# Which queue issues the last three stores of a kernel

## The chip, the cores and the metric

The kernel runs on one core of one Trainium2 chip. Five engines work side by side on it: TensorE (PE in the profile, with its weight loads as PEld), VectorE (DVE), ScalarE (ACT), GpSimd (POOL) and SyncE (SP). Transfers between the chip's memory (HBM) and the core's working memory (SBUF) are DMAs: an engine issues one from its own stream of instructions, and the packets are then moved by 16 DMA engines. In this kernel SP issues nearly all of them (queue q1 in the profile) and ACT a few (q10).

The metric is the device time of one execution in microseconds (us). A profiled execution also has a span, from its first instruction to its last, which is a little shorter than its time.

## The reference

From x of 2048 rows and 640 columns, in bf16, the result is the sum of x and two branches that share one layer norm:

```python
xn = _layernorm(x)
return x + _A_ref(xn, A_wqkv, A_wo) + _B_ref(xn, B_w_gate, B_w_up, B_w_down)

# A: 32 heads of 20, each row sees itself and the 255 rows before it
qkv = (x @ wqkv).reshape(B, S, 3, H, Dh)
scores = einsum("bhqd,bhkd->bhqk", q, k) * (Dh ** -0.5)   # masked to the window
o = einsum("bhqk,bhkd->bhqd", softmax(scores), v)
A = o.reshape(B, S, D) @ wo

# B: 1536 hidden columns
h = sigmoid(xn @ w_gate) * (xn @ w_up)
B = h @ w_down
```

## The kernel before

The 2048 rows are worked in four chunks of 512, and a chunk in four row blocks of 128. For each chunk the kernel normalises and transposes the rows, projects q, k and v, forms the scores and their exponentials in steps, multiplies them with v, and computes the gated branch into tiles `h`. The order of all instructions is written out by hand (`tc.manual_schedule()`): the main loop (lines 757 to 778) interleaves the score steps with other work that it pulls from a list, so that TensorE always has something to do. The output of the first three chunks is part of that list.

The output of the last chunk stands behind the loop, from line 782 on, and the change lies there. The output of a row block needs, for each cut of its columns, twelve matmuls of `h` with the down weights (`down`, line 470) and five of the attention result with `wo` (`add_wo`, line 477), all summed in one bank of PSUM, the memory that TensorE writes. `add_x` (line 481) is one VectorE instruction that halves the sum and adds x, in place, in the tile that holds x's rows. `store` (line 493) then writes those columns to `out` on a queue that it is given. For the first three row blocks the cuts are two halves of 320 columns, and one store of 160 KB on SP's queue takes both (`outp`). The tile of the last row block is not called `rows` in the profile, but `xn`: it lies in the buffer `xns["last"]`, whose rows ACT loads some 20 us before the end (line 790).

The last row block has three cuts, of 320, 256 and 64 columns (line 800), and each is added and stored by itself as soon as its sum is there: 80 KB, 64 KB and 16 KB. The twelve `down` matmuls of the first two cuts are issued ahead of time (lines 808 and 809), those of the third inside the loop. That loop, lines 812 to 817, names the queue of each store. An engine works through its instructions in order, so a store waits on its engine both for the data and for whatever the engine has ahead of it.

After the stores the program ends (the profile's line 841): SP waits for the outstanding stores one after the other, drains, and the engines meet.

Of the kernel before, what the change touches and what calls it, by code (L numbers as in the profile page):

```python
# [93 lines left out]
def kernel(  # L94
# [11 lines left out]
    nc = tc.nc  # L106
# [368 lines left out]
    def add_wo(c, s, y, cut):  # L475
        for m in range(DC):
            nc.tensor.matmul(y[:, 0:cut[1] - cut[0]], lhsT=oc[c, m][:, s * P:(s + 1) * P],  # L477
                             rhs=wo[:, m, cut[0]:cut[1]], start=False, stop=(m == DC - 1))

    def add_x(y, cut, rows):  # L480
        nc.vector.scalar_tensor_tensor(  # L481
            out=rows[:, cut[0]:cut[1]], in0=y[:, 0:cut[1] - cut[0]], scalar=0.5,
            in1=rows[:, cut[0]:cut[1]], op0=MULT, op1=ADD)
# [7 lines left out]
    def store(c, s, rows, cut=(0, D), queue=nc.sync):  # L491
        sb = c * SBC + s
        queue.dma_start(out=out2[sb * P:(sb + 1) * P, cut[0]:cut[1]], in_=rows[:, cut[0]:cut[1]])

    def outp(c, s, ys, rows):
        for y, cut in zip(ys, HALVES):
            add_wo(c, s, y, cut)
        for y, cut in zip(ys, HALVES):
            add_x(y, cut, rows)
        store(c, s, rows)  # L500
# [251 lines left out]
    cuts = [(ends[n, NG - 2] + 2 + n, f"out{n}") for n in range(NCH - 1)] + [(len(todo), None)]  # L752
# [42 lines left out]
    def add_down(s, cut, home, tag):  # L795
        ys[s, cut] = home.tile([P, CW], FP32, name="y0", tag=tag)
        run(down(c, s, ys[s, cut], cut))

    last = SBC - 1
    cuts = (HALVES[0], (HALF, D - U), (D - U, D))  # L800
# [8 lines left out]
    add_down(last, cuts[1], ps_d, "d")  # L809
    for s in range(1, last):  # L810
        outp(c, s, [ys[s, cut] for cut in HALVES], rows[s])
    for cut, queue in zip(cuts, (nc.scalar, nc.sync, nc.scalar)):
        if cut == cuts[2]:
            add_down(last, cut, ps_y, "y")
        add_wo(c, last, ys[last, cut], cut)
        add_x(ys[last, cut], cut, rows[last])
        store(c, last, rows[last], cut, queue)
# [28 lines left out]
```

## Time and profile before

| | |
|---|---|
| three runs | 308.06, 308.20 and 308.88 us, median 308.2 |
| the profiled execution | 308.24 us |
| its span, first to last instruction | 306.4 us |
| granted TensorE clock over the span | 1.00 |
| PE busy | 302.0 us, 99% of the span |
| ACT busy | 198.5 us, 65% |
| DVE busy | 177.7 us, 58% |
| POOL busy | 177.5 us, 58% |
| stores of the last row block | `out_dram<-xn`, 80 KB on ACT's queue, 64 KB on SP's, 16 KB on ACT's |

In the profile a line such as `303.07 0.35 ACTq L493 DMA_DIRECT2D out_dram<-xn x1` is a DMA that ACT issued from line 493: it started at 303.07 us from the span's start, and the issue (not the transfer) occupied ACT's stream for 0.35 us. `SPq` is the same for SP. `out_dram<-xn` says that `out` is written from the tile `xn`. An `EVENT_SEMAPHORE` is an instruction that waits for, or sets, a counter through which engines and DMAs tell each other that something is done; its time is shown once the wait is over. A line of the waits, `SPq L841 <- DMA out_dram<-xn: 0.4, 2, 0.2`, says that SP's stream waited at line 841 for DMAs of that kind, 0.4 us in all, twice, 0.2 us at the longest. In the DMA view a line such as `q10 hardware_dynamic: 8, 0.00, 12.5%` gives a queue's packets in a window, their megabytes, and the share of 16 engines' time that they took; `q8` and `q14` (kind `instruction`) are fetches of the program itself.

### The profile page before, as it was taken

What the parts mean: (1) busy time and instruction counts of PE and PEld (TensorE: products, weight loads), DVE (VectorE), ACT (ScalarE), POOL (GpSimd) and SP (SyncE); (2) the same over time, 40 slices, a digit from 0 to 9 for tenths busy, and PEclk for the clock granted to TensorE, in tenths of its full rate; (3) what the DMA queues carried; (4) which work ended last, traced back from release to release, by engine and by line L of the source; (5) the groups of instructions that cost most, each with busy time, mean ns of one, the idle gap of its engine ahead of it and who ended that gap; (6) DMA issues with size and microseconds to landing.
All of it is one profiled execution on the core that took longest, in us unless ns stands there. A gap on an engine that the chain in (4) does not pass through costs nothing.

```text
span 306.4 us, 10028 instructions
## 1 busy us (share of the span) xinstructions
PE 302.0 (99%) x4314; PEld 164.8 (54%) x4314; DVE 177.7 (58%) x355; ACT 198.5 (65%) x197; POOL 177.5 (58%) x317
## 2 busy tenths in 40 slices
PE   7999999999999999999999999999999999999996
PEld 3654444445657644554457654554546664444774
DVE  5735539879675564497946464483733526372534
ACT  6933877698854649888674647878585547778000
POOL 3174686787982828576682728557382847557000
PEclk9999999999999999999999999999999999999999
DMA  7998987986537062810036212740000210000202
GB/s 206 361 325 266 303 199 213 318 229 192 175 97 166 21 180 70 273 40 2 2 132 131 66 58 87 231 144 0 2 2 2 71 40 25 2 2 2 88 21 68
DMA packets 40174, 36.87 MB, mean 120 GB/s; under 512 B 8864, under 2 KB 39840, under 8 KB 40096
## 3 DMA queue, kind: packets, MB, share of 16 engines
q1 hardware_dynamic: 39264, 35.46, 38.2%
q10 hardware_dynamic: 864, 0.75, 0.8%
q8 instruction: 34, 0.56, 0.8%
q14 instruction: 12, 0.10, 0.1%
HBM read 25.59 MB, written 11.44 MB: 121 GB/s over the span
## 4 chain that ended last, share of the span: by engine, by line
PE 97%; DMA 1%; ACT 1%; DVE 0%; SPq 0%; issue 0%
PE y L470 18%; PE pu L456 18%; PE pg L449 17%; PE pqk L324 15%; PE ps L526 9%; PE pv L353 7%; PE y L477 7%; PE acc L559 6%; DMA xc<-in_A_x_dram 1%; PE pt L277 0%; ACT xn L656 0%; ACT xn L661 0%; DVE xn L667 0%; SPq L156 0%; ACT rstd L662 0%
## 5 line engine op out<-in xcount | busy, mean ns | idle before, releaser
L543 POOL TENSOR_SCALAR_AFFINE_SELECT pT<-pT 64x512 bf16<-64x512 bf16 (+1 forms) x256 | 157.4, 615 | 83.0 <-ACT pT L532 70.5
L532 ACT ACTIVATE pT<-ps 128x2048 bf16<-128x2048 f32 (+1 forms) x76 | 141.0, 1855 | 59.4 <-PE ps L526 56.0
L460 DVE SCALAR_TENSOR_TENSOR h<-th,pu 128x512 bf16<-128x512 f32 x48 | 32.6, 680 | 49.7 <-PE pu L456 44.2
L456 PE MATMUL pu<-xnT,wu 128*128 128x512 bf16 x240 | 59.8, 380 | 0.0
L449 PE MATMUL pg<-xnT,wg 128*128 128x512 bf16 x240 | 59.8, 380 | 0.0
L470 PE MATMUL y<-wd,h 128*128 128x320 bf16 (+2 forms) x396 | 56.6, 295 | 0.0
L470 PEld LDWEIGHTS <-h 128*128 128x128 bf16 x396 | 36.7, 98 | 15.8 <-issue 1.8
L452 ACT ACTIVATE th<-pg 128x512 f32<-128x512 f32 x48 | 28.6, 595 | 15.5 <-PE pg L449 15.4
L449 PEld LDWEIGHTS <-wg 128*128 128x128 bf16 x240 | 22.2, 98 | 25.8 <-issue 1.8
L456 PEld LDWEIGHTS <-wu 128*128 128x128 bf16 x240 | 22.0, 98 | 25.5 <-issue 2.0
L526 PE MATMUL ps<-qT,kT 20*64 20x320 bf16 (+4 forms) x1440 | 32.1, 260 | 0.0
L571 DVE STREAM_TRANSPOSE t<-acc 128x512 f32<-128x512 f32 x32 | 21.1, 696 | 17.3 <-PE acc L559 17.3
L526 PEld LDWEIGHTS <-kT 20*64 20x64 bf16 x1440 | 15.4, 103 | 25.0 <-issue 22.4
L481 DVE SCALAR_TENSOR_TENSOR rows<-y,rows 128x320 bf16<-128x320 f32 x30 | 14.5, 488 | 22.8 <-PE y L477 22.7
L583 DVE TENSOR_TENSOR on<-t,rec 128x320 bf16<-128x320 f32 (+4 forms) x48 | 26.1, 543 | 1.1
L353 PE MATMUL pv<-wv,xnT 128*128 128x320 bf16 x160 | 25.7, 300 | 0.0
L477 PE MATMUL y<-wo,oc 128*128 128x320 bf16 (+2 forms) x165 | 24.2, 295 | 0.0
L324 PE MATMUL pqk<-xnT,wq 128*128 128x512 bf16 x100 | 23.2, 380 | 0.0
L324 PE MATMUL pqk<-xnT,wk 128*128 128x512 bf16 x100 | 23.1, 380 | 0.0
L364 DVE CAST v<-pv 64x320 bf16<-64x320 f32 x29 | 14.1, 486 | 11.7 <-PE pv L353 11.4
L559 PE MATMUL acc<-pT,v 64*32 64x320 bf16 (+4 forms) x1440 | 19.6, 253 | 0.0
L559 PEld LDWEIGHTS <-v 64*32 64x32 bf16 x1440 | 16.2, 91 | 5.8 <-issue 1.6
(53 smaller groups left out, 194.7 us busy)
## 6 DMA issues: line engine op xcount, KB each, us to landing
qT<-sq SPq DMA_DIRECT2D x16, 256.0 KB
kT<-sk SPq DMA_DIRECT2D x16, 256.0 KB
sq<-st SPq DMA_DIRECT2D x20, 128.0 KB
sk<-st SPq DMA_DIRECT2D x20, 128.0 KB
out_dram<-rows SPq DMA_DIRECT2D x15, 160.0 KB
wg<-in_B_w_gate_dram SPq DMA_DIRECT2D x4, 480.0 KB
wu<-in_B_w_up_dram SPq DMA_DIRECT2D x4, 480.0 KB
xc<-in_A_x_dram SPq DMA_DIRECT2D x3, 640.0 KB
```

The lines of the kernel that those rows point to most:

```text
L324: nc.tensor.matmul(ps, lhsT=wt[:, m, :], rhs=xnT[c][:, d, :], start=(d == 0), stop=(d == DC - 1))
L353: nc.tensor.matmul(ps[:, 0:HALF], lhsT=xnT[c][:, d, s * P:(s + 1) * P], rhs=wqkv[2][:, d, hf * HALF:(hf + 1) * HALF], start=(d == 0), stop ...
L449: nc.tensor.matmul(pg, lhsT=part(wg, d, f), rhs=xnT[c][:, d, :], start=(d == 0), stop=(d == DC - 1))
L452: nc.scalar.activation(out=th, in_=pg, func=TANH, scale=0.5)
L456: nc.tensor.matmul(pu, lhsT=part(wu, d, f), rhs=xnT[c][:, d, :], start=(d == 0), stop=(d == DC - 1))
L460: nc.vector.scalar_tensor_tensor(out=h, in0=th, scalar=1.0, in1=pu, op0=ADD, op1=MULT)
L470: nc.tensor.matmul(y[:, 0:cut[1] - cut[0]], lhsT=ht[c, f][:, s * P:(s + 1) * P], rhs=wd[:, f, cut[0]:cut[1]], start=(f == 0), stop=False)
L477: nc.tensor.matmul(y[:, 0:cut[1] - cut[0]], lhsT=oc[c, m][:, s * P:(s + 1) * P], rhs=wo[:, m, cut[0]:cut[1]], start=False, stop=(m == DC - 1))
L526: nc.tensor.matmul(ps[a * U:(a + 1) * U, i, col * U:(col + n) * U], lhsT=qk["k", kc, o // GH][32 * i:32 * i + DH, o % GH + a, kb * U:(kb + ...
L532: nc.scalar.activation(out=pt[:, :, 0:width], in_=ps[:, :, 0:width], func=EXP, scale=SCALE)
L543: nc.gpsimd.affine_select(out=view, in_=view, pattern=[[0, HG], [0, n], [sign, U]], compare_op=GE, fill=0.0, base=base, channel_multiplier ...
L559: nc.tensor.matmul(acc[32 * i:32 * i + 32, q * U:(q + n) * U], lhsT=vt[kb][a * U:(a + 1) * U, u, h * VW:h * VW + 32], rhs=pt[a * U:(a + 1) ...
```

## The change

The three stores of the last row block keep their order, sizes and data. The first goes from ACT's queue to SP's, the second from SP's to ACT's, the third stays on ACT's. SP thus issues one of the three and ACT two, as before, but ACT's two now come one directly after the other.

```diff
     for s in range(1, last):
         outp(c, s, [ys[s, cut] for cut in HALVES], rows[s])
-    for cut, queue in zip(cuts, (nc.scalar, nc.sync, nc.scalar)):
+    for cut, queue in zip(cuts, (nc.sync, nc.scalar, nc.scalar)):
         if cut == cuts[2]:
             add_down(last, cut, ps_y, "y")
         add_wo(c, last, ys[last, cut], cut)
```

## The prediction

> **What bounds the kernel now.** I read the page from its parts 1, 2 and 4 down, to learn which engine carries the span and which one its end, and then the last four microseconds instruction by instruction. The page's rows of busy time, of ACT and POOL in 40 slices, of the ACT queue (q10), and of the chain by engine:
>
> ```profile
> PE 302.0 (99%) x4314; PEld 164.8 (54%) x4314; DVE 177.7 (58%) x355; ACT 198.5 (65%) x197; POOL 177.5 (58%) x317
> ...
> ACT  6933877698854649888674647878585547778000
> POOL 3174686787982828576682728557382847557000
> ...
> q10 hardware_dynamic: 864, 0.75, 0.8%
> ...
> PE 97%; DMA 1%; ACT 1%; DVE 0%; SPq 0%; issue 0%
> ```
>
> TensorE is the bound: 97% of the chain. The change touches no matmul, and everything it touches comes after or beside the last matmuls. ACT's last three slices (from 283.4 us) show 0: it computes next to nothing there, and its stream has stores to issue. The end of the chain of waits, then the timeline of the same stretch (start us, length us):
>
> ```profile
> 303.06 0.35 PE y L470 x12
> 303.41 0.16 PE y L477 x5
> 303.57 0.02 issue
> 303.59 0.23 DVE xn L481
> ```
>
> ```profile
> 302.39 0.33 SPq L493 DMA_DIRECT2D out_dram<-rows  x1
> 302.55 0.49 DVE L481 SCALAR_TENSOR_TENSOR xn<-y,xn 128x320 bf16<-128x320 f32 x1 [0.19 <-PE y L477]
> ...
> 303.07 0.35 ACTq L493 DMA_DIRECT2D out_dram<-xn  x1
> 303.10 0.72 DVE L481 SCALAR_TENSOR_TENSOR xn<-y,xn 128x256 bf16<-128x256 f32 x2
> ...
> 303.55 0.49 SPq L493 DMA_DIRECT2D out_dram<-xn  x1
> 303.59 0.23 DVE L481 SCALAR_TENSOR_TENSOR xn<-y,xn 128x64 bf16<-128x64 f32 x1
> 303.85 0.35 ACTq L493 DMA_DIRECT2D out_dram<-xn  x1
> ```
>
> Call the three stores A (320 columns, 80 KB), B (256, 64 KB) and C (64, 16 KB). Each is issued 0.03 us after its add on VectorE ends (303.04, 303.52, 303.82): at 303.07, 303.55 and 303.85. SP's issues of the other row blocks take 0.33; B took 0.49. What follows C, from the instructions of the kernel's last line (L841) and from SP's waits over the last ten microseconds:
>
> ```profile
> L841 SPq EVENT_SEMAPHORE  x2: 28/28/28, 304.9 to 305.2; - x2
> ...
> L841 SPq DRAIN  x3: 7/7/13, 305.6 to 305.9; - x3
> ```
>
> ```profile
> SPq L841 <- DMA out_dram<-rows: 0.8, 1, 0.8
> ...
> SPq L841 <- DMA out_dram<-xn: 0.4, 2, 0.2
> ```
>
> SP waits for the stores in the order of the program, the row block before the last first (0.8 us, until 304.9), then A, B and C, and at 305.6 it drains: the last wait is for C (the same rows in narrower windows put the ends of the waits for A, B and C at 305.2, 305.4 and 305.6). From C's issue to that drain lie 305.6 - 303.85 = 1.75 us, from the drain to the span's end 306.4 - 305.6 = 0.8 us.
>
> **The change part by part.** The sum is made against the profiled execution's own 308.24 us, which is 306.4 of span and 1.84 around it; the median of the runs shown is 308.2, so the two agree to 0.04.
>
> A moves from ACT to SP. SP ended its previous issue at 302.39 + 0.33 = 302.72 and is idle, so A is still issued at 303.07 and SP is free again by 303.40 (at 0.33) or 303.56 (at 0.49). Its packets now stand in q1 behind those of the 160 KB store issued at 302.39, and the last wait for that one ends at 304.9 against A's 305.2. Should A be late by some tenths, B's and C's waits (305.4, 305.6) cover it. Cost nothing; with that cover gone it would cost what A lands past 305.6. SP's later instructions are waits alone, for landings long after 303.56.
>
> B moves from SP to ACT. ACT is idle: its last compute instruction ended before 284. B is issued at 303.55 as before, for 0.35 us (both ACT stores took that) instead of 0.49. B landing 0.14 earlier earns nothing, C being waited for last.
>
> C stays on ACT, but now stands behind B there, and this is the only step on the path. Its data is ready at 303.82, ACT only after B. The price is the spacing of two ACT issues one after the other. The trace shows it in the four loads that ACT issues at 282.75, 283.25, 283.73 and 284.13: 0.50, 0.48 and 0.40 us apart, the last pair with no semaphore instruction between, the others with one of 38 ns. Between A and C stands one of 17 ns, and I expect it between B and C: 0.35 + 0.017 + two gaps of about 0.04 (283.25 + 0.36 = 283.61 to 283.73 is 0.12, less 0.038, so 0.04 a side) = 0.45. C is then issued at 303.55 + 0.45 = 304.00 instead of 303.85: 0.15 late. From both sides: 0.40 gives 0.10 late, and 0.50, with B's 0.14 of stretch moving along to ACT, gives 0.29. I take 0.15, the value of the spacing nearest in form.
>
> What follows C moves with it: the 1.75 us to the drain, the 0.8 to the end. Its lower side is set by the DMA engines, where C's small packets met B's. The DMA view of 304.5 to 304.7, of 304.7 to 304.95, and of 304.95 to 305.7 (share is of 16 engines over the window):
>
> ```profile
> DMA packets 84, 0.04 MB, mean 215 GB/s; under 512 B 1, under 2 KB 84, under 8 KB 84
> ```
>
> ```profile
> DMA packets 205, 0.04 MB, mean 165 GB/s; under 512 B 156, under 2 KB 205, under 8 KB 205
> ```
>
> ```profile
> DMA packets 6, 0.02 MB, mean 22 GB/s; under 512 B 4, under 2 KB 4, under 8 KB 4
> ...
> q14 instruction: 2, 0.02, 8.6%
> ```
>
> C's rows are 128 bytes, so they start at about 304.7, 0.85 after the issue, and are through by 304.95, B's among them. With B issued in 0.35 its packets come 0.14 earlier and are gone when C's arrive. If C's packets, alone then, take 0.1 instead of 0.25 us, the delay of 0.15 is won back: the lower end of the step is 0. I keep 0.15, because C's start is what the issue sets, and that is the row I can read.
>
> [...] In the rows B's issue (303.55 to 304.04) and C's (303.85 to 304.20) overlap by 0.19, C's is no longer than A's, and its packets come 0.85 after its start as A's do (window 303.9 to 303.95 has A's first); only B's stretch by 0.16 looks like sharing. [...]
>
> Sum: 308.24 + 0 (A) + 0 (B) + 0.15 (C) = 308.39, with 0 and 0.29 as ends, 308.24 to 308.53.
>
> **The rivals.** "No change" here means within 0.3%, 0.92 us, about what a measurement of this kernel can tell from no change: 307.28 to 309.12.
>
> First, an instruction fetch falls on C. The last window above has two fetches of 8 KB (q14), 8.6% of 16 x 0.75 us = 1.03 us of one engine between them, the first beginning within 0.04 us of that window's start, right behind C's last packets. C's last packets, 0.15 later, reach to about 305.1, and the fetches, which I take to follow SP's passing of the wait at 304.9, don't move. On an engine that has a fetch and rows of C, C waits for 0.5 us, or for 1.03 if one engine takes both first. Speaking for it: a 16 KB fetch (q8, 3.0% of 16 x 2.2 = 1.06 us between 302.3 and 304.5) lies beside the 160 KB store that was issued at 302.39 and landed only at 304.9, where A, issued 0.68 later and half as large, landed at 305.2. Against it: a share of C is eight rows on an engine, and may be through. With one fetch 308.24 + 0.15 + 0.5 = 308.9, still no change; with both 308.24 + 0.15 + 1.03 = 309.4, slower. It decides from 0.77 us on top of C's 0.15.
>
> Second, slower: ACT holds C until B has landed, by a wait placed between two stores of one tile on one queue. B takes from its issue to SP's wait for it 305.4 - 303.55 = 1.85; C would be issued at about 305.4 instead of 303.85, 1.55 later: 309.8. Against it: A and C are two stores of that tile on that queue already, the semaphore instruction between them takes 17 ns, and C was issued at 303.85 when A landed at 305.2.
>
> Third, a small gain: B out of C's way is worth more than the 0.15, and C lands up to 0.1 earlier than before: 308.1, no change. [...] A gain over 0.92 has no place: of the 1.75 us from C's issue to the drain, 0.85 passes before its first packet and about 0.6 after its last (304.95 to 305.55), and B's route changes neither.
>
> That the edit does nothing would need C to be issued at 303.85 all the same; ACT can't, with B on it from 303.55 to 303.90 and the semaphore instruction behind it.
>
> **How the numbers follow.** The forecast has 0.62. Its own range is 308.1 to 308.6: 308.24 to 308.53 with the 0.04 between profile and median and a tenth for the runs' scatter. The fetch has 0.16: 0.12 with one (308.9) and 0.04 with both (309.4). C held for B has 0.06 (309.8), the small gain or nothing lost 0.08 (308.1 to 308.24). What no row here shows has 0.08: 0.04 slower, and 0.04 faster, which is how far a median of few runs can stray when three runs of one kernel spread from 308.06 to 308.88. So slower 0.04 + 0.06 + 0.04 = 0.14, faster 0.04, no change 0.62 + 0.12 + 0.08 = 0.82. The predicted time is 308.4. The range goes from 307.9, below the small gain by the scatter, to 309.1, over one fetch by the same; outside are the 0.14 slower and about 0.04 below.
>
> **What would show it right or wrong.** In the timeline after: A as an SP issue at 303.07; B on ACT at 303.55 for 0.35; C on ACT at 303.95 to 304.05. C at 303.85 or a B of 0.49 would put the step wrong. In SP's waits: the row block before the last still until 304.9, A near 305.2, B near 305.25, C last, and the drain at about 305.75. A drain at 306.2 or later with the packets on time is the fetch; C's issue past 305 is the hold. A's wait as the last one would say that A behind the 160 KB store isn't covered. All of TensorE's rows, and everything before 303, should stand as they are; if the span moves there, the prediction's premise is wrong.

## The result, and the profile after

| | before | after |
|---|---|---|
| median of the runs | 308.16 us (9 runs, 307.88 to 308.94) | 309.27 us (9 runs, 309.11 to 310.25) |
| profiled execution | 308.24 us | 309.23 us |
| its span | 306.4 us | 307.4 us |

The change makes the kernel slower, by a ratio of 1.0034 with a 95% interval of 1.0021 to 1.0046: about 1 us. The forecast was no change, 308.4 us, in a range of 307.9 to 309.1. The time lies 0.17 us above that range.

The page's rows of busy time, the two rows in 40 slices, the ACT queue and the chain by engine, after the change:

```profile
PE 300.5 (98%) x4279; PEld 165.1 (54%) x4314; DVE 178.2 (58%) x355; ACT 198.4 (65%) x197; POOL 176.6 (57%) x317
...
ACT  6933877698855649887774547888585647687000
POOL 3174686787982828575673729467372937565000
...
q10 hardware_dynamic: 864, 0.74, 0.8%
...
PE 98%; issue 1%; DVE 0%
```

Nothing in them tells where 1 us went. (PE's matmuls number 4279 instead of 4314 because records are missing; its weight loads are all there.) The end of the chain of waits, over the last five microseconds, shows that all the work before the stores is where it was:

```profile
303.08 0.35 PE y L470 x12
303.43 0.16 PE y L477 x5
303.59 0.02 issue
303.61 0.23 DVE xn L481
```

C's add ends at 303.84 instead of 303.82. So the loss comes after it. The timeline after, whole and then cut so that ACT's two issues stand apart (start us, length us):

```profile
302.41 0.33 SPq L493 DMA_DIRECT2D out_dram<-rows  x1
...
303.09 1.06 SPq L493 DMA_DIRECT2D out_dram<-xn  x1
303.57 0.83 ACTq L493 DMA_DIRECT2D out_dram<-xn  x2
```

```profile
303.57 0.35 ACTq L493 DMA_DIRECT2D out_dram<-xn  x1
```

```profile
304.02 0.39 ACTq L493 DMA_DIRECT2D out_dram<-xn  x1
```

Two things are new. A's issue on SP lasts 1.06 us, and C is issued at 304.02 instead of 303.85. Then SP's waits over the last ten microseconds, and the last line's instructions in the window around the drain:

```profile
SPq L841 <- DMA out_dram<-xn: 1.3, 2, 0.9
...
SPq L841 <- DMA out_dram<-rows: 0.8, 1, 0.8
```

```profile
L841 SPq DRAIN  x2: 7/7/7, 306.6 to 306.7; - x2
```

The row block before the last is waited for as long as before (0.8 us). A wait for one of the last three stores has grown from 0.2 to 0.9 us: it is the last one, for C, and the drain comes at 306.6 instead of 305.6. That is the whole microsecond. What held C stands in the DMA view, in the windows 304.9 to 305.2 and 305.2 to 305.6:

```profile
DMA packets 192, 0.05 MB, mean 164 GB/s; under 512 B 151, under 2 KB 191, under 8 KB 191
...
q14 instruction: 1, 0.01, 6.8%
```

```profile
DMA  0000000000000000000000000000000000000000
GB/s 0 0 0 0 0 0 0 0 0 0 0 0 0 0 0 0 0 0 0 0 0 0 0 0 0 0 0 0 0 0 13 13 13 13 13 13 13 13 0 0
DMA packets 9, 0.00 MB, mean 3 GB/s; under 512 B 9, under 2 KB 9, under 8 KB 9
```

In the first window the rows of C pass on 15 of the 16 DMA engines (120 of its 128 rows, and 15 of the 16 packets of 4 bytes that come behind them), and a program fetch of 8 KB (q14) begins in its last slices: 6.8% of 16 x 0.3 us = 0.33 us of one engine, from 305.18 on. In the second window there is silence for 0.3 us, and then nine small packets, from 305.50 to 305.59: the eight rows of C that are left (one engine's share of the store), and the last packet of 4 bytes. In the kernel before, the last of C's packets ended at 304.98 by the trace's packet records, and the fetch began 0.006 us after it. After the change C's packets on the 15 other engines ended 0.21 later, at 305.191, and the fetch itself began 0.20 later, at 305.185. So by these times alone the margin is as thin as before, on the other side; the records don't name the engine, and what moved the fetch they don't show. What they do show is that the late rows waited for the fetch: it ended at 305.509, and the first of the eight rows began at 305.505. In four of the runs below in which C came late, its eight rows begin in the same way, 0.003 to 0.004 us before the end of the fetch.

The landing was late too. In the trace's records of landings, the last share of C landed at 305.55 before, 0.57 us behind C's last packet. After the change it landed at 306.56, 0.97 behind it. The sum: 0.17 (issue) + 0.44 (the last rows, 305.59 - 304.98 less the 0.17) + 0.40 (landing) = 1.01, against 1.00 between the two landings.

### The profile page after: what moved, and what is told of

It is laid out like the page before. It is cut to its first block, busy times and chain, and to the rows that moved or that the text cites. A ratio compares the mean times of both kernels' runs of the same rounds, so it can differ in the third digit from the quotient of the medians.

```text
span 307.4 us, 9993 instructions
## 1 busy us (share of the span) xinstructions
PE 300.5 (98%) x4279; PEld 165.1 (54%) x4314; DVE 178.2 (58%) x355; ACT 198.4 (65%) x197; POOL 176.6 (57%) x317
## 4 chain that ended last, share of the span: by engine, by line
PE 98%; issue 1%; DVE 0%
PE y L470 18%; PE pu L456 17%; PE pg L449 17%; PE pqk L324 14%; PE ps L526 9%; PE pv L353 7%; PE y L477 7%; PE acc L559 6%; PE pwarm L226 2%; PE pt L277 1%; DVE xn L481 0%
## 5 line engine op out<-in xcount | busy, mean ns | idle before, releaser
L456 PE MATMUL pu<-xnT,wu 128*128 128x512 bf16 x228 | 59.0, 380 | 0.7 <-issue 0.2
L449 PE MATMUL pg<-xnT,wg 128*128 128x512 bf16 x226 | 58.5, 380 | 0.9 <-issue 0.3
```

The costliest lines, as they stand in the source:

```text
L449: nc.tensor.matmul(pg, lhsT=part(wg, d, f), rhs=xnT[c][:, d, :], start=(d == 0), stop=(d == DC - 1))
L456: nc.tensor.matmul(pu, lhsT=part(wu, d, f), rhs=xnT[c][:, d, :], start=(d == 0), stop=(d == DC - 1))
```

## The experiments

What had to be told apart: theory D, that C's later issue alone puts its share behind the fetch; theory H, that A's held issue on SP is needed for it; theory F, that the fetch is what costs the time; and rival S, that the stores get in each other's way and the fetch is a bystander. The first four runs set D against H and look for the owner of the fetch.

**One half of the change: B to ACT, A stays.**

```diff
-    for cut, queue in zip(cuts, (nc.scalar, nc.sync, nc.scalar)):
+    for cut, queue in zip(cuts, (nc.scalar, nc.scalar, nc.scalar)):
```

> Half of the change: B goes to ACT, A stays on ACT, so ACT issues all three stores. Theory H (the held issue): the 1.0 us comes from A on SP, whose issue lasted 1.06 us because the 160 KB store ahead of it on SP's queue was stuck on one DMA engine behind a 16 KB program fetch; A's late packets then push C's share on that engine behind the two 8 KB fetches at the end. With A on ACT no issue is held: A at 303.07 and B at 303.55 for 0.35 each, C at 304.0, drain at about 305.75, 308.35 us. Theory D (C's delay alone): C issued 0.17 later is enough to fall behind the fetches; it is issued at 304.0 here too, so its last landing is again near 306.5 and the time 309.2.

Measured: 309.12 us, ratio 1.0023 (1.0014 to 1.0033). H as stated falls: A was issued on ACT for 0.35 us, and the loss is there. It isn't a clean case for D, though, since C was issued 0.52 us behind its add and not 0.18 (304.46): B's issue took 0.41, and C's began only at the moment when the last rows of the 160 KB store had passed (304.45). Two fetches began at 305.13 and 305.21, before C's first packet at 305.31.

**The other half: A to SP, B stays.**

```diff
-    for cut, queue in zip(cuts, (nc.scalar, nc.sync, nc.scalar)):
+    for cut, queue in zip(cuts, (nc.sync, nc.sync, nc.scalar)):
```

> The other half: A goes to SP, B stays on SP, C alone on ACT and issued at 303.85 as in the kernel before. Theory H: A's issue on SP lasts about 1.06 us again (until 304.15), B is issued behind it at about 304.2 instead of 303.55, and A and B land late: between 308.7 and 309.3 us, with B and not C as the last wait. Theory D: C is not delayed, so the time is the one before, 308.2, or at most 308.5 if B lands 0.3 later than C did.

Measured: 309.42 us, ratio 1.0032 (1.0020 to 1.0044). A's issue lasted 0.82 us, B came behind it and was the last wait. C, issued 0.03 behind its add, landed 1.49 us after its issue, the shortest of all. B's last rows stood behind a fetch at 305.53. So each half alone costs about a microsecond, by a different store. D had said 308.2 to 308.5 here and H 308.7 to 309.3 with B as the last wait, so H was the nearer; neither had B's rows meeting the fetch. (In this profile 0.32 us of the loss isn't the stores': everything from about 210 us on is that much later than in the kernel before.)

**C on SP behind B.**

```diff
-    for cut, queue in zip(cuts, (nc.scalar, nc.sync, nc.scalar)):
+    for cut, queue in zip(cuts, (nc.scalar, nc.sync, nc.sync)):
```

> The kernel before with C on SP behind B, so that ACT issues A alone and is through at 303.42. It tells whose the two 8 KB fetches near the end are. If they are ACT's (they begin 0.75 us behind ACT's drain in the kernel before and 0.74 in the changed one), they come at about 304.2, ahead of B and C. If they are SP's (0.07 and 0.09 us behind the end of SP's wait for the 160 KB store), they stay near 305.0. B's issue on SP is held until 304.04 as in the kernel before (0.49 us), so C is issued at about 304.1, 0.25 later than before: 308.45 us where the fetches don't meet it, by both theories; 309.2 where they do.

Measured: 309.13 us, ratio 1.0028 (1.0019 to 1.0036). C was issued at 304.03 and its last share landed at 306.44. The two fetches came apart: one stayed at 305.10, the other moved to 307.86, past the end of the span. ACT had one store less, two instructions fewer, so the second fetch goes by how far ACT has come in its program. The first was neither ACT's by its drain (303.48, now 1.6 us ahead of it) nor, as it turned out, SP's. The run also bears on D: A was issued on ACT for 0.35 us and B on SP for 0.41, much as in the kernel before, and C, 0.19 us behind its add, had its eight last rows behind the fetch and brought the whole loss. That is a delay of the changed kernel's size without A's held issue, though with C on another queue.

**The changed kernel with TensorE's fetch moved away from A.**

```diff
-    keep_busy((CW,) * 6)
+    keep_busy((P,) * 24)
```

> The changed kernel with the 16 KB program fetch of TensorE moved away from the 160 KB store: the first six of the 512-column matmuls that keep TensorE busy at the start become 24 of 128 columns, which adds 36 TensorE instructions at about the same work and should bring each of TensorE's fetches 36 instructions earlier, at the end by some 2.3 us (from 302.8 to about 300.5). The result is unchanged. Theory H: the store ahead of A is no longer stuck, A's issue on SP lasts 0.33 to 0.35 instead of 1.06 us, its packets start at 303.9, and the time falls to 308.35 us. Theory D: C is still issued at 304.0, and the time stays at 309.2.

Measured: 310.55 us, ratio 1.0069 (1.0052 to 1.0086). The edit itself costs 1.4 us: C's add ends at 305.21 instead of 303.84. They are not lost at the start, where the edit is, but at about 203 us, where TensorE stands still for 1.2 us before its matmuls of line 526; the profile gives `issue` as what it waited for, so the reason is open. Less the 1.4 us the time is about 309.15, as D said. The end can be read for itself all the same. From the timeline:

```profile
303.78 0.33 SPq L493 DMA_DIRECT2D out_dram<-rows  x1
304.46 0.33 SPq L493 DMA_DIRECT2D out_dram<-xn  x1
304.94 0.84 ACTq L493 DMA_DIRECT2D out_dram<-xn  x2
```

With the 16 KB fetch at 301.27 and no longer near the 160 KB store, A's issue takes 0.33 and not 1.06 us, and that store's 16 shares land within 0.19 us of each other instead of 1.08. So the 16 KB fetch is what held A's issue; that part of H is shown. The other runs agree: in all twelve profiles in which the fetch lay beside that store and SP had another one to issue, A or B, that issue ended 0.37 to 0.42 us behind the end of the fetch. But C, issued at 305.39, still had its last share land 2.48 us later (2.54 in the changed kernel, 1.71 in the kernel before), behind a fetch at 306.39. The held issue isn't what costs the time.

**The changed kernel with twelve VectorE instructions more.**

```diff
     outp(c, 0, [ys[0, cut] for cut in HALVES], rows[0])
+    pad = const.tile([P, 1], FP32, name="pad")
+    for _ in range(12):
+        nc.vector.memset(pad, 0.0)
```

> The changed kernel with twelve one-column VectorE instructions put behind the adds of the last chunk's first row block (about 296.8 us, where VectorE is idle for 3 us). Theory F (the fetch): VectorE fetches 8 KB of program each time it has gone some 128 instructions further (by the counts at the earlier fetches, near its 65th, 191st, 321st and 447th), the last time just behind its last add, and that fetch takes C's turn on one DMA engine. With twelve more instructions ahead it comes at about 297.5 instead, C's packets pass, and C lands 0.6 and not 0.97 us behind its last packet: 308.35 us. Rival S (the stores alone): C's lateness comes from A's and B's packets and from C's issue behind B, which stay: 309.2. If the fetch that C meets is ScalarE's, it stays 309.2 as well, and the ScalarE pads of the next run move it.

Measured: 308.37 us, ratio 1.0003 (0.9994 to 1.0013). The loss is gone. The timeline has the same stores as the changed kernel, A's held issue too:

```profile
296.65 1.46 DVE L810 MEMSET pad<- 128x1 f32 x12
...
303.06 0.84 SPq L493 DMA_DIRECT2D out_dram<-xn  x1
303.55 0.84 ACTq L493 DMA_DIRECT2D out_dram<-xn  x2
```

The DMA view from 304.8 to 305.3 has all of C's rows, where the changed kernel has nine packets left over:

```profile
DMA packets 219, 0.05 MB, mean 96 GB/s; under 512 B 169, under 2 KB 219, under 8 KB 219
```

SP drains at 305.7. The fetch is at 293.5, earlier than I had said (297.5) and ahead of the twelve instructions themselves (296.65 on). VectorE had then started 434 recorded instructions, where the kernel before had started 447 at its last fetch, so a plain count doesn't place it, and why it comes so early stays open. C was issued at 303.99 and landed at 305.64, 0.09 later than in the kernel before: that is the price of the delay with the fetch out of the way. So theory F holds and S falls, and the fetch is VectorE's, in that VectorE's instructions move it.

**The changed kernel with twelve ScalarE instructions more.**

```diff
     rows.append(new_rows(c, SBC - 1, xns["last"][:, 0, :], nc.scalar))
+    for _ in range(12):
+        nc.scalar.activation(out=scr, in_=neghalf[:, 0:1], func=EXP)
```

> The changed kernel with twelve one-column ScalarE instructions behind the four loads that ScalarE issues, at about 285 us, where it is idle. They bring ScalarE's own 8 KB fetch (near its 319th instruction, its last) forward to about 286. Theory F with VectorE as owner of the first of the two fetches: one fetch stays near 305.2, C still loses its turn: between 308.9 and 309.2 us. Theory F with ScalarE as its owner: 308.35. Rival S: 309.2.

Measured: 309.21 us, ratio 1.0034 (1.0022 to 1.0046). ScalarE's fetch went to 286.0, one fetch stayed, at 305.05, and C's last rows came behind it. This is the control of the run above: as many idle instructions, on the engine whose fetch is harmless, and the loss stays. It also shows that one fetch costs all of it.

**The changed kernel with both pads, and the kernel before with both.** In the one and in the other, both hunks from above:

```diff
+    for _ in range(12):
+        nc.vector.memset(pad, 0.0)
...
+    for _ in range(12):
+        nc.scalar.activation(out=scr, in_=neghalf[:, 0:1], func=EXP)
```

> The changed kernel with both pads: no program fetch between 303.9 and the end. Theory F, whoever owns which fetch: C, issued at 304.0 behind B, lands at about 305.7 and the time is 308.35, 0.15 over the kernel before, which is what C's later issue alone costs. Rival S: 309.2.

> The kernel before with both pads. Theory F: C was already ahead of the fetch there by some thousandths of a us, so the usual run stays at 308.2; the occasional runs at 308.6 to 309.4 of the kernel before are those where C met it, and they should go. Rival S: 308.2, with the occasional higher runs as before.

Measured: 308.38 us, ratio 1.0002 (0.9990 to 1.0014), and 308.42 us, ratio 1.0005 (0.9996 to 1.0015). Without the fetch the two orders of the stores can't be told apart. My other expectation was wrong: the kernel before with the pads still has runs up to 308.96. In its profile (308.91 us) the tail from the 160 KB store on is 0.85 us later as a whole, 303.24 instead of 302.39. Nearly all of that is there by 11.5 us, where a VectorE copy starts 0.79 us later than in the kernel before. So this higher run was lost near the start and not at the stores; what causes it stays open.

**The kernel before with two VectorE instructions more.** The stores are untouched.

```diff
+    for _ in range(2):
+        nc.vector.memset(pad, 0.0)
```

> The kernel before, stores untouched, with two instead of twelve VectorE instructions behind the adds of the last chunk's first row block. Theory F: VectorE's 8 KB fetch follows by about 1.4 to 1.5 us the instruction at which it falls due, so two instructions more bring it forward from C's add to B's, from 304.99 to about 304.5, ahead of C's packets (304.73 to 304.98) and no longer just behind them. On the engine that fetches, C is late by 0.3 to 0.5 us, and its landing comes up to 0.35 later behind its packets than without a fetch: 308.6 to 309.1 us with the stores of the kernel before, C issued 0.03 us behind its add as always. Rival, that the fetch matters only together with the changed order of the stores: 308.3.

Measured: 308.31 us, ratio 1.0003 (0.9994 to 1.0012). It doesn't tell the two apart, because the fetch missed C again: it came at 303.05, 0.5 us behind the start of A's add and not at 304.5, and met the 160 KB store, of which a second share landed late (304.87). C's packets ran from 304.71 to 304.94 with no fetch in them.

**C alone made late, first attempt, without and with the VectorE pad.** Two ScalarE instructions between A's and C's issue, beside the twelve of the control:

```diff
         store(c, last, rows[last], cut, queue)
+        if cut == cuts[1]:
+            for _ in range(2):
+                nc.scalar.activation(out=scr, in_=neghalf[:, 0:1], func=EXP)
```

> The kernel before with its stores on their queues (A on ACT, B on SP, C on ACT), but two one-column ScalarE instructions of 0.23 us each between A's and C's issue, so that C is issued at about 304.0 as in the changed kernel; and the twelve ScalarE pads at 285 us, which by themselves gained nothing and keep ScalarE's own fetch out of the way. Theory D with F (C's delay alone puts its share behind VectorE's fetch): C's packets start 0.15 later, the fetch at about 305.0 comes first on one engine, and C lands at about 306.4: 309.1 us. Theory H with F (it needs A's held issue on SP, whose late packets are ahead of C): the fetch comes behind C, 308.35.

> The same with the twelve VectorE pads as well, which bring VectorE's fetch forward to about 293.5. Both theories: C issued at 304.0 with no fetch near it lands at about 305.7, 308.35 us; were it 309.1, the delay of C would cost 0.9 by something other than the fetch.

Measured: 308.42 us, ratio 1.0004 (0.9990 to 1.0018), and 308.23 us, ratio 0.9989 (0.9977 to 1.0001). Nothing follows for D, since the delay didn't come about: C was issued 0.03 us behind its add. The first run is of use as the control of the next one, though, with the same twelve ScalarE instructions: its fetch began at 305.31, 0.11 behind the last of C's packets (305.20), and C landed 1.64 us behind its issue. In this run C's add ended at 304.07 and ACT issued C at 304.10, while its own instruction was still running until 304.17:

```profile
303.73 0.44 ACT L822 ACTIVATE scr<-neghalf 128x1 f32<-128x1 f32 x2 [16.06 <-DVE xn L481]
304.10 0.35 ACTq L493 DMA_DIRECT2D out_dram<-xn  x1
```

**C alone made late, second attempt.** Now C's data itself depends on a ScalarE instruction (with the twelve ScalarE instructions of the control above):

```diff
         add_x(ys[last, cut], cut, rows[last])
+        if cut == cuts[2]:
+            end = rows[last][:, cut[0]:cut[1]]
+            nc.scalar.copy(out=end, in_=end)
```

> The kernel before with its stores on their queues, but ScalarE copies C's 64 columns onto themselves between C's add and C's issue, so that C alone waits for one ScalarE instruction more: issued 0.25 to 0.4 late, at 304.1 to 304.25, with nothing else ahead of it on ACT's queue than A; and the twelve ScalarE pads at 285 us as in the run of that name. Theory D with F (C's delay alone is enough to lose the turn to VectorE's fetch): the fetch at about 305.0 stands ahead of C's rows on one engine, C's last landing at about 306.4 to 306.5: 309.1 us. Theory H with F (it needs A on SP or B ahead of C on ACT): only the delay itself, 308.5.

Measured: 309.29 us, ratio 1.0030 (1.0020 to 1.0040). A on ACT for 0.35 us, B on SP for 0.39, C issued 0.31 us behind its add:

```profile
303.13 0.35 ACTq L493 DMA_DIRECT2D out_dram<-xn  x1
303.60 0.39 SPq L493 DMA_DIRECT2D out_dram<-xn  x1
303.90 0.24 ACT L821 COPY xn<-xn 128x64 bf16<-128x64 bf16 x1 [16.44 <-DVE xn L481]
304.18 0.35 ACTq L493 DMA_DIRECT2D out_dram<-xn  x1
```

The DMA view from 305.3 to 306.5 again has nine small packets, behind a fetch at 305.08:

```profile
DMA packets 9, 0.00 MB, mean 1 GB/s; under 512 B 9, under 2 KB 9, under 8 KB 9
```

The last landing is at 306.52. With the stores on the queues of the kernel before, C's delay alone brings the whole loss. So D holds, here for a delay of 0.28 us and in the run with C on SP for 0.16. This kernel with VectorE's fetch moved away was not tried; that the fetch is the cause here too rests on the order in the trace.

The seven profiles that decide, side by side (issue behind the add and landing behind the issue by the trace's records):

| kernel | C issued behind its add | fetch ahead of C's last rows | C's last landing behind its issue | median |
|---|---|---|---|---|
| before | 0.03 us | no (0.006 us behind) | 1.71 us | 308.16 us |
| after | 0.18 | yes | 2.54 | 309.27 |
| after, VectorE pad | 0.18 | no | 1.65 | 308.37 |
| after, ScalarE pad | 0.18 | yes | 2.47 | 309.21 |
| after, both pads | 0.18 | no | 1.65 | 308.38 |
| before, C on SP | 0.19 | yes | 2.42 | 309.13 |
| before, C held by a copy | 0.31 | yes | 2.34 | 309.29 |

No kernel tried beats the kernel before: the lowest median, 308.23, has an interval that reaches 1.0001.

## Why the prediction was wrong

**What bounds the kernel.** Right. TensorE's end and the three adds moved by 0.02 us, and the loss lies wholly behind them.

**A.** Issued at 303.09, as forecast. Its issue was expected to last 0.33 to 0.49 us and lasted 1.06, because SP's queue was held by the 160 KB store, one share of which stood behind TensorE's 16 KB fetch (302.83 to 303.78) and landed at 305.07, the other fifteen by 304.19 (0.33 without that fetch). B's 0.49 in the kernel before, which I read as a sign of two engines sharing something, was the same hold: B too was on SP behind that store, and its issue ended 0.41 us behind the end of the 16 KB fetch, as it did within 0.38 to 0.42 in the six other runs with B in that place. "Cost nothing" was right: A landed at 305.54 and not near 305.2, and C's wait covered it. With the VectorE pad A is held for 0.84 us and the time is that of the kernel before.

**B.** Right: issued at 303.57 for 0.35 us, landed by 305.30 (forecast 305.25), worth nothing.

**C's issue.** Right: 304.02, forecast 304.00.

**"What follows C moves with it: the 1.75 us to the drain".** This is the step that failed. From C's issue to the drain it was 306.64 - 304.02 = 2.62 us, 0.87 more than the term. I took the stretch behind the issue to be rigid. It wasn't here: VectorE's 8 KB program fetch came just ahead of C's last rows and put them 0.44 us and their landing another 0.40 us later. With the fetch moved away the term is 305.72 - 303.99 = 1.73, and the time 308.37, against the forecast's 1.75 and 308.39. The lower end of the step, the delay won back because C's packets find B's gone, didn't come about either: B's were gone by 304.79, but A's, held back on SP, ran among C's until 305.10, and C's on 15 engines took 0.23 us instead of 0.25.

**The first rival** named the right mechanism, and from the right row: the fetch that began right behind C's last packets. Three things about it were wrong. Its chance was set at 0.16, although C's delay (0.15) was far longer than the gap in front of the fetch (0.04 as read, 0.006 in the packet records; that the fetch would come 0.20 later too could not be read from the kernel before), with only "a share of C is eight rows and may be through" against it. Its price was 0.5 for one fetch; measured it was 0.44 for the rows and 0.40 for the landing. And the owner was wrong: the fetch doesn't follow SP's wait, it moves with VectorE's instructions (to 293.5 with twelve more). The landing is a part of the price that the rival didn't have: with the fetch ahead, C's last share landed 0.97 us behind its last packet (0.84 in the control and 0.83 in the copy run), without it 0.57 before and 0.51 with the VectorE pad. Why it took longer with the fetch ahead was not shown.

**The hold for B's landing** didn't happen: one 17 ns semaphore instruction stood between B and C. **Sharing between two issues** doesn't show in B's issue either: after the change B's issue on ACT (303.57 to 303.92) lies wholly inside A's 1.06 us on SP, and takes its usual 0.35. **Nothing lost** (308.24, in the 0.08 of the small gain) rests on nothing that a run shows: C was issued 0.17 us later than before, and in the run with the fetch out of the way, issued 0.14 later, it landed 0.09 later.

**The range** ended at 309.1 with the rival priced at 308.9. Priced at 309.2, and given the larger part of the chance, it would have been the forecast.

## What to carry to other kernels

A delay at the very end of this kernel cost no more than its own length (C issued 0.14 us and landed 0.09 us later, with the VectorE pad) only as long as nothing overtook; with the fetch ahead, 0.17 us of it became 1.0 us. Look in the DMA view at what comes in the next few tenths behind the last packets, program fetches included, and compare that gap with the delay before calling the delay small. When a tail reacts out of proportion, add a dozen idle instructions on one engine: here they moved that engine's fetch (VectorE's from 305.19 to 293.5, ScalarE's from 305.81 to 286.0), and the run on VectorE showed that its fetch was the cause. The same number on another engine is the control.

## What the runs showed of the hardware

- The two 8 KB program fetches at the end moved each with the instructions of one engine. The first stayed at 305.05 with twelve ScalarE instructions more, and went to 293.5 with twelve on VectorE; in the kernel before two on VectorE moved it from 304.99 to 303.05. The second went to 286.0 with twelve on ScalarE, and to 307.86 with two fewer (C on SP). In the kernel before, four of the 8 KB fetches stand near VectorE's 65th, 191st, 321st and 447th recorded instruction (45.8, 114.5, 202.4 and 305.0 us), 126 to 130 apart. With the twelve the last one came after the 434th, so the count alone doesn't say where. Where it fell against the stores thus changed with instructions that have nothing to do with them.
- TensorE's 16 KB fetch beside the 160 KB store held the next DMA issue of SP's queue: A's issue took 0.82 to 1.06 us against 0.33 without the fetch, and ended 0.37 to 0.38 us behind the end of the fetch.
- In the first attempt to delay C, ACT issued it at 304.10, 0.03 us behind its add, while ACT's own instruction ahead of it was still running until 304.17: the two idle instructions ahead of the issue didn't delay it. The instruction that produced the data did (C issued 0.31 us behind its add in the copy run). So the store waited there for the instructions ahead of it to be issued, not for the end of their work.
